# Retention, soft MoE and gated MLP on one core: the hand-over from the experts to the last product rewritten

## Chip, cores and metric

The kernel runs on one core of one Trainium2 chip. The metric is the device time of one execution in microseconds (us). Engines are named as in the profile: PE (matmuls) and PEld (its weight loads), DVE, ACT, POOL, and SP, whose queue issues most DMAs.

## The reference, cut to what matters

```python
attn = retention(q, k, v)                       # 4 x 8 heads x 768 tokens x 64
x = attn as 3072 tokens x 512
logits = x @ phi                                # 32 slots, 8 experts of 4 slots
d = softmax(logits over tokens); slot_input = d.T @ x
slot_out[e] = relu(slot_input[e] @ w1[e]) @ w2[e]
x = softmax(logits over slots) @ slot_out       # c @ slot_out
h = x @ w_in                                    # 512 -> 2048
out = (h * sigmoid(1.702 * h)) @ w_out          # 2048 -> 512
```

w_in and w_out are float64, and the kernel narrows them itself. The product x @ w_in is never formed through x: with G = slot_out @ w_in (32 x 2048), h is c @ G, so a block of h costs one matmul with the router's transposed weights c.

## The kernel before, in words

**Stages.** Attention runs first (to about 110 us of the span), then the experts in four pairs (`exp_w1` L484, `exp_t1` L498, `exp_w2` L507, `exp_t2` L523), then the last product, which fills the rest from about 159 us on.

**Experts.** `exp_w2(ep)` accumulates a pair's output in PSUM and copies it to `os` on ACT (L520). All pairs share one tile `eo` of two banks, pair `ep` taking bank `ep % 2` (L511). `exp_t2(ep)` turns `os` with 8 PE passes (`tq`) and lets DVE write the scaled result into `soT4`, which lies in tile A (L529). After pair 3, `make_gd(f)` (L536) can make 128 columns of G from `soT4` and `win`: 8 PE passes, an ACT copy (L541) and a DVE subtraction (L542) into `gst`.

**Narrowing.** A weight arrives as 64-bit words, and three DVE passes (`narrow`, L157: L160, L162, L164, called n1, n2, n3 below) make it float32. For a row block of w_out (`wout_ops`, L575), ACT then rounds a high part (L582) and POOL makes the low part (L585); later blocks are done in pairs by ACT and DVE. `wout_ops(0)` and `wout_ops(1)` are run by hand around the hand-over, `win_ops(0, 0, ...)` in two halves. Three buffers (`wq`, L86) hold raw weights, so a load on SP's queue waits until the pass n3 of an earlier raw tile is over.

**Router transposes.** `tr_cT(g)` (L422) turns the router weights of 512 tokens with four PE passes, and `copy_cT(g)` (L428) copies them into `cT` on ACT. Groups 0 to 2 are turned before the last product, groups 3 to 5 in its steps s = 7, 8 and 9 (L1143, L1144).

**Last product.** A unit u is a pair (b, f): a block b of 512 tokens and a row block f of w_out. `h_unit(u)` (L662) is one 128x512 matmul, then two ACT activations: `gh` (rounded, L674) and `gg` (L675). `lo_unit(u)` (L678) is the DVE subtraction `gl = gg - gh` (L680). `o_unit(u)` (L700) adds 12 matmuls of 512 columns into four accumulators: for each of four token tiles t, the terms (gh, w high), (gh, w low) and (gl, w high). Units 0 and 1 are block 0, 2 to 5 block 1, 6 to 9 block 2. Unit 0 runs term by term over the four tiles, all others tile by tile (L717, L724). The accumulators rotate over banks 0 to 4 (`acc_bank`), so the first unit of a block takes one free bank and three that the block before it must leave. `h_bank()` rotates over banks 5 to 7.

After a block's last unit, ACT copies the four accumulators into four buffers `sg` (L728, L732), and `store_sums()` (L690) has DVE subtract within two of them (L694) and sends all four to DRAM (L696). For block 0 these four DMAs are issued by ACT's own queue, in program order between its instructions. The next block's `sg` copies wait until the stores have landed.

**Order.** The order is written out by hand. Up to s = 4 it stands in L1085 to L1115. From s = 5 on, the loop at L1130 does `h_unit(s)`, a budget of weight preparation (`work`), `lo_unit(s)` and `o_unit(s - 2)`; at s = 5 `o_unit` is left out, as unit 3 is done already. `work(budget)` takes items off a queue, each with a cost written beside it, and carries an overdraft to the next call. Its items are, in order: the six narrowing passes of the third quarter of w_in (`b1`, L1042), w_out blocks 2 and 3 (`first_pair`, with two POOL passes at step 4), then the raw tiles wi1_0 and wi1_1 (three passes of 1024 columns each), and so on. At s = 5 block 0's sums are stored first thing (L1136).

**Idle passes.** `keep_warm(n)` (L480) issues n matmuls whose result nobody reads: 2, 1 and 2 of them (KW, L49) before `exp_t2(3)`, before `make_gd(0)` and before `h_unit(0)`.

Of the kernel before, what the change touches and what calls it, by code (L numbers as in the profile page):

```python
# [22 lines left out]
P = 128  # L23
# [22 lines left out]
I0 = 1  # L46
KTP = (0, 1, 2, 3, 8, 13, 16, 20)
PAD = 128
KW = (2, 1, 2)  # L49
BUD = 2.0  # L50
E0 = (1.2, 1.7, 1.7, 1.7, 2.2)
WL = (3, 2)
# [3 lines left out]
def retention_soft_moe_mlp(  # L56
# [418 lines left out]

    hT_t, H_p, O_p = {}, {}, {}

    kw = {}

    def keep_warm(n, cols=512):  # L480
        for _ in range(n):
            mm(kw["out"][:, 0:cols], lhsT=kw["in"][0], rhs=kw["in"][1][:, 0:cols], start=True, stop=True)

    def exp_w1(ep, k0=0, k1=KDM):  # L484
        if k0 == 0:
            H_p[ep] = ps.tile([P, 512], F32, tag=f"sc{ep % 2}", name=f"hp{ep}")
# [20 lines left out]
    def exp_w2(ep, k0=0, k1=4):  # L507
        if k0 == 0:
            if ep == 0:
                O_p["all"] = ps.tile([P, 2, 512], F32, tag="y", name="eo")  # L510
            O_p[ep] = O_p["all"][:, ep % 2]  # L511
        op, hT = O_p[ep], hT_t[ep]
        for kk in range(k0, k1):
            w = W["w2", ep, kk]
            for j in range(4):
                mm(op[32 * j:32 * j + 32, :], lhsT=hT[:, kk, 32 * j:32 * j + 32], rhs=w[:, j, :],  # L516
                   start=(kk == 0), stop=(kk == 3))
        if k1 == 4:
            os_ = xk.tile([P, 512], F32, tag="os", name=f"os{ep}", bufs=1)
            nc.scalar.copy(out=os_, in_=op)  # L520
            O_p[ep] = os_
# [53 lines left out]
    def wout_ops(f):  # L575
        r, c = f // 2, slice(f % 2 * DM, f % 2 * DM + DM)
        w = fr_tile(r)[:, c]
        h, l = w_t[r][:, 0, f % 2], w_t[r][:, 1, f % 2]
        n1, n2, n3 = narrow(w.bitcast(U32), raw_words(wo_t[r])[:, c])

        def hi():
            nc.scalar.copy(out=h, in_=w)  # L582

        def lo():
            nc.gpsimd.tensor_tensor(out=l, in0=w, in1=h.bitcast(F32), op=ALU.subtract)  # L585
            wh[f], wl[f] = h, l

        return [n1, n2, n3, hi, lo]
# [37 lines left out]
    def win_ops(j, z, k0=0, k1=KDM, f0=0, f1=256):  # L626
        raw = raw_t[j, z].bitcast(U32).rearrange("p k (f z) -> p k f z", z=2)
        if j not in win:
            win[j] = rw.tile([P, KDM, 512], F32, tag="win", name=f"win{j}", bufs=1)
        return narrow(win[j][:, k0:k1, 256 * z + f0:256 * z + f1].bitcast(U32), raw[:, k0:k1, f0:f1])  # L630
# [20 lines left out]
    def flat(i):  # L651
        return pb[:, i].rearrange("p z c -> p (z c)")
# [25 lines left out]
    def lo_unit(u):  # L678
        gg, gh, gl = g_hl[u]
        nc.vector.tensor_tensor(out=gl, in0=gg, in1=gh.bitcast(F32), op=ALU.subtract)  # L680
# [19 lines left out]
    def o_unit(u, t0=0, t1=4, terms=(0, 1, 2)):  # L700
        kind, (b, f) = seq[u]
        _, gh, gl = g_hl[u]
        whi, wlo = wh[f], wl[f]
        first = (b, f) in firsts
        last = kind == "p" and (b, f) in lasts
        final = u == NSEQ - 1
        ops = [(gh, whi), (gh, wlo), (gl, whi)]
        if first and 0 in terms:
            for t in range(t0, t1):
                acc[t] = acc_bank() if kind == "p" else flat(QBANK[t])  # L710

        def term(t, n):
            g, w = ops[n]
            mm(acc[t], lhsT=g[:, t * P:(t + 1) * P], rhs=w, start=first and n == 0,  # L714
               stop=n == 2 and (last or final or (u == NSEQ - 2 and t == 3)))

        if u == 0:  # L717
            for n in terms:
                for t in range(t0, t1):
                    term(t, n)  # L720
        if final:
            add_out(3, 0, 2, acc[3], store=False)
        for t in range(t0, t1 - 1 if final else t1):
            if u > 0:  # L724
                for n in terms:
                    term(t, n)
            if last:
                sg = fp.tile([P, DM], F32, tag="sg", name=f"sg{b}_{f}_{t}", bufs=4)  # L728
                if t % 2 and u == NP1 - 1:
                    nc.vector.tensor_copy(sg, acc[t])  # L730
                else:
                    nc.scalar.copy(out=sg, in_=acc[t])  # L732
                if u == NP1 - 1 and t in (1, 2):
                    s_load(0, t - 1)
                stores.append((scr[b][:, t], sg, t % 2 == 0, (b, f + 1) in seconds or b not in twice,
                               nc.sync if u == NP1 - 1 else nc.scalar if u == 1 else nc.gpsimd))
            if final:
                add_out(t, 0, 2, acc[t])
        if final:
            for n_, c in enumerate((slice(0, 256), slice(256, 512))):  # L740
                rest = flat(4 + n_)
                for n, (g, w) in enumerate(ops):
                    mm(rest[:, c], lhsT=g[:, 3 * P:4 * P], rhs=w[:, c], start=n == 0, stop=n == 2)
                add_out(3, n_, n_ + 1, rest)
# [71 lines left out]
    with tc.manual_schedule():  # L816
# [127 lines left out]
            WA[j] = wp.tile([P, 3, 2, 256], F32R, tag="w", name=f"wa{j}")  # L944
            WB[j] = wp.tile([P, 4, 2, 256], F32R, tag="w", name=f"wb{j}")
        load_wout(1)
        kw["in"] = cT[:, 0:128], cT
        nc.gpsimd.memset(selhl.bitcast(F32), 0.0)
        exp_t2(1)
        cp = [tr_cT(0, ps.tile([P, 4, P], F32R, tag="m", name="cp0", bufs=3))]  # L950
# [7 lines left out]
                    selhl[:, z, :, 64 * z + 32 * r:64 * z + 32 * r + 32], ident.rearrange("p (c s) -> p c s", c=4)  # L958
                )
        exp_w2(2)  # L960
        f0_ops = wout_ops(0)
        exp_w2(3, 0, 1)
        exp_t2(2)
        for fn in f0_ops:
            fn()
        exp_w2(3, 1, 4)
        cp = {g: tr_cT(g, ps.tile([P, 4, P], F32R, tag="m", name=f"cp{g}", bufs=3)) for g in (1, 2)}
        kw["out"] = ps.tile([P, 512], F32, tag="sc0", name="kw1")
        keep_warm(KW[0])
        exp_t2(3)  # L970
        for g in (1, 2):
            copy_cT(g, cp[g])
        w1_ops = win_ops(0, 0, f0=128)
        w1_ops[0]()
        w1_ops[1]()
        keep_warm(KW[1])
        make_gd(0, ps.tile([P, P], F32, tag="st", name="gd0"))
        w1_ops[2]()
        f1_ops = wout_ops(1)
        f1_ops[0]()  # L980
        f1_ops[1]()
        keep_warm(KW[2])
        xk_e.close()
        sm_e.close()
        ps_e.close()
# [53 lines left out]

            todo.append(make)  # L1040

        b1 = [x for p_ in zip(win_ops(0, 1, 0, 2), win_ops(0, 1, 2, 4)) for x in p_]  # L1042
        b1[-1] = used(b1[-1])
        todo.append(lambda: queue.extend(zip((0.4, 0.4, 0.7, 0.7, 0.7, 0.7), b1)))
        def first_pair():
# [36 lines left out]
                for fn in later.pop(x):  # L1082
                    fn()

        kw["out"] = flat(4)  # L1085
        h_unit(0)
        lo_unit(0)
        for fn in f1_ops[2:4]:
            fn()
        o_unit(0, terms=(0,))  # L1090
        make_gd(1, h_bank()[:, 0:P])
        f1_ops[4]()
        o_unit(0, terms=(1,))
        h_unit(1)
        work(E0[0])
        lo_unit(1)
        o_unit(0, terms=(2,))
        h_unit(2)
        work(E0[1])
# [30 lines left out]
        for s in range(5, NSEQ + 2):  # L1130
# [2 lines left out]
            u, nxt_ = s - 2, s + 1  # L1133
            if kind == "p":
                h_unit(s)
            if s == 5:  # L1136
                store_sums()
            if kind == "p":
                work(BUD - (0.8 if stores else 0))
                lo_unit(s)  # L1140
            store_sums()
            if kind == "p":
                if s in (7, 8, 9):  # L1143
                    copy_cT(s - 4, tr_cT(s - 4, h_bank().bitcast(F32R).rearrange("p (j t) -> p j t", j=4)))  # L1144
            if s == NP1 - 1:
                work(1000)
                for x in range(s, s + 9):
# [131 lines left out]
```

## Time and profile before

| | |
|---|---|
| median of 3 runs | 454.88 us (454.49 to 455.13) |
| profiled execution | 454.33 us |
| its span | 452.6 us (1.73 us lie around it) |
| busy: PE, DVE, ACT, POOL | 97%, 72%, 47%, 16% of the span |
| granted clock of TensorE | 1.00 (the full 2.4 GHz) |

The profile is of one execution. A row of the timeline gives the start in us from the span's beginning, the length, engine, source line, operation, out<-in, the shape and the count, and in brackets the idle time ahead of it with what ended that. Matmuls overlap, so the distance between starts is what one costs; a queue row (SPq, ACTq) is an issue of a DMA.

### The profile page before, as it was taken

What the parts mean: (1) busy time and instruction counts of PE and PEld (TensorE: products, weight loads), DVE (VectorE), ACT (ScalarE), POOL (GpSimd) and SP (SyncE); (2) the same over time, 40 slices, a digit from 0 to 9 for tenths busy, and PEclk for the clock granted to TensorE, in tenths of its full rate; (3) what the DMA queues carried; (4) which work ended last, traced back from release to release, by engine and by line L of the source; (5) the groups of instructions that cost most, each with busy time, mean ns of one, the idle gap of its engine ahead of it and who ended that gap; (6) DMA issues with size and microseconds to landing.
All of it is one profiled execution on the core that took longest, in us unless ns stands there. A gap on an engine that the chain in (4) does not pass through costs nothing.

```text
span 452.6 us, 10122 instructions
## 1 busy us (share of the span) xinstructions
PE 439.4 (97%) x4128; PEld 365.3 (81%) x4128; DVE 327.6 (72%) x624; ACT 214.2 (47%) x386; POOL 70.3 (16%) x81
## 2 busy tenths in 40 slices
PE   8999999999899989999999999999999999999996
PEld 5887877888333467788878878999999999999994
DVE  2455665765465488988778777798888999998835
ACT  2223233232121264673655657565666666665630
POOL 4344444443000112101130230000000000000000
PEclk9999999999999999999999999999999999999999
DMA  8999999999899657865576243503321333303102
GB/s 316 406 401 403 402 398 397 396 402 337 327 423 400 257 196 269 248 218 185 187 221 149 95 60 82 184 4 94 94 94 44 100 99 94 107 30 92 49 0 93
DMA packets 31630, 94.50 MB, mean 209 GB/s; under 512 B 3104, under 2 KB 10432, under 8 KB 28000
## 3 DMA queue, kind: packets, MB, share of 16 engines
q1 hardware_dynamic: 28176, 85.99, 51.6%
q0 software_dynamic: 2544, 6.46, 6.0%
q10 hardware_dynamic: 864, 1.41, 0.9%
q8 instruction: 32, 0.52, 0.5%
q14 instruction: 14, 0.11, 0.1%
HBM read 79.17 MB, written 14.68 MB: 207 GB/s over the span
## 4 chain that ended last, share of the span: by engine, by line
PE 87%; DMA 6%; DVE 5%; issue 1%; ACT 1%; DVEq 0%; ACTq 0%
PE pb L779 31%; PE pb L714 22%; DMA qt<-qt_dram 6%; PE sc L208 5%; PE y L257 4%; PE eo L516 3%; PE hp L491 3%; PE pb L753 3%; PE y L253 2%; PE pb L665 2%; PE xp L278 2%; PE st L265 1%; PE op L372 1%; PE wu L832 1%; PE kp L219 1%
## 5 line engine op out<-in xcount | busy, mean ns | idle before, releaser
L779 PE MATMUL pb<-wb,ghl 128*128 128x256 f32 x672 | 100.7, 283 | 0.0
L714 PE MATMUL pb<-wo_hl,gh 128*128 128x512 f32 x288 | 91.0, 398 | 0.7 <-ACT gh L674 0.7
L779 PEld LDWEIGHTS pb<-wb,ghl 128*128 128x128 f32 x672 | 89.5, 192 | 0.0
L779 PE MATMUL pb<-wa,ghl 128*128 128x256 f32 x504 | 78.9, 283 | 0.0
L779 PEld LDWEIGHTS pb<-wa,ghl 128*128 128x128 f32 x504 | 68.7, 192 | 0.0
L714 PEld LDWEIGHTS pb<-wo_hl,gh 128*128 128x128 f32 x288 | 53.5, 188 | 13.0 <-ACT gh L674 1.0
L768 DVE TENSOR_TENSOR ghl<-F,ghl 128x896 fp32r<-128x896 f32 x56 | 60.6, 1084 | 0.1
L756 ACT ACTIVATE F<-pb 128x512 f32<-128x512 f32 x56 | 33.5, 598 | 52.2 <-PE pb L753 52.2
L714 PE MATMUL pb<-wo_hl,gl 128*128 128x512 f32 x144 | 56.6, 397 | 1.2 <-DVE gl L680 1.2
L764 ACT CAST ghl<-F 128x896 fp32r<-128x896 f32 x56 | 52.3, 934 | 1.4 <-DVE F L760 1.4
L212 DVE TENSOR_TENSOR pt<-sc,ca_t 128x512 f32<-128x512 f32 x44 | 28.3, 686 | 19.2 <-PE sc L208 19.2
L680 DVE TENSOR_TENSOR gl<-gg,gh 128x512 fp32r<-128x512 f32 x36 | 24.8, 688 | 16.3 <-ACT gg L675 16.2
L674 ACT ACTIVATE gh<-pb 128x512 fp32r<-128x512 f32 x36 | 21.7, 603 | 29.6 <-PE pb L665 27.6
L714 PEld LDWEIGHTS pb<-wo_hl,gl 128*128 128x128 f32 x144 | 27.2, 189 | 8.6 <-DVE gl L680 2.1
L758 DVE TENSOR_TENSOR F<-F 128x256 f32<-128x256 f32 x56 | 23.6, 422 | 14.0 <-ACT F L756 13.8
L234 POOL TENSOR_TENSOR tb<-ca_t 128x512 f32<-128x512 f32 x19 | 19.9, 1048 | 42.8 <-DVE xT L269 42.8
L208 PEld LDWEIGHTS sc<-qt,ktv 64*128 64x128 f32 x320 | 19.8, 187 | 7.8 <-issue 4.5
L267 ACT COPY s_sb<-st 128x256 f32<-128x256 f32 x20 | 7.5, 372 | 38.5 <-PE st L265 38.5
L208 PE MATMUL sc<-qt,ktv 64*128 64x128 f32 x320 | 23.7, 284 | 1.3 <-DMA qt<-qt_dram 1.1
L257 PE MATMUL y<-pt,vt 128*64 128x128 f32 x352 | 24.1, 279 | 0.0
L226 POOL TENSOR_TENSOR vt<-ktv,ca_t 128x512 f32<-128x512 f32 x20 | 20.9, 1042 | 12.2 <-PE xp L278 6.5
L753 PE MATMUL pb<-cT,gst 128*128 128x256 f32 x112 | 22.6, 284 | 0.0
(188 smaller groups left out, 653.2 us busy)
## 6 DMA issues: line engine op xcount, KB each, us to landing
w<-w_dram SPq DMA_DIRECT2D x36, 512.0 KB, 7.4
w<-w_dram SPq DMA_DIRECT2D x14, 1024.0 KB, 8.3
ktv<-ktv_dram SPq DMA_DIRECT2D x20, 512.0 KB, 8.3
wi<-w_in_dram SPq DMA_DIRECT2D x7, 1024.0 KB, 5.0
wo<-w_out_dram SPq DMA_DIRECT2D x7, 1024.0 KB, 4.9
scr<-sg POOLq DMA_DIRECT2D x24, 256.0 KB, 3.5
pr<-scr SPq DMA_DIRECT2D x12, 512.0 KB, 5.0
qt<-qt_dram SPq DMA_DIRECT2D x21, 256.0 KB, 6.4
```

Of the source, the lines that this page charges most:

```text
L208: mm(sc[hh][:, a, :], lhsT=kT[hh * D:(hh + 1) * D, a, :], rhs=q_[hh * D:(hh + 1) * D, a, :], start=True, stop=True)
L212: nc.vector.tensor_tensor(out=pt[hh], in0=sc[hh], in1=mask[:, None, :].to_broadcast([P, NP, P]), op=ALU.mult)
L257: mm(out_(a, hh ^ (a & 1)), lhsT=vt[:, 2 * a + (hh ^ (a & 1)), :], rhs=pt[hh ^ (a & 1)][:, a, :], start=(c == 0 and a < 2), stop=True, ski ...
L674: nc.scalar.activation(out=gh, in_=hp, func=AF.Gelu_apprx_sigmoid)
L680: nc.vector.tensor_tensor(out=gl, in0=gg, in1=gh.bitcast(F32), op=ALU.subtract)
L714: mm(acc[t], lhsT=g[:, t * P:(t + 1) * P], rhs=w, start=first and n == 0, stop=n == 2 and (last or final or (u == NSEQ - 2 and t == 3)))
L753: mm(hp[:, 256 * z:256 * z + 256], lhsT=gst[:, (f + z) * P:(f + z + 1) * P], rhs=cT[:, 256 * blocks[e]:256 * blocks[e] + 256], start=z == ...
L756: nc.scalar.activation(out=F[:, 0:4].rearrange("p q t -> p (q t)"), in_=hp, func=AF.Gelu_apprx_sigmoid)
L758: tt(out=F[:, 4:6], in0=F[:, 0, None].to_broadcast([P, 2, P]), in1=F[:, 1:3], op=ALU.subtract)
L764: nc.scalar.copy(out=GHL[k][:, 0], in_=F_[k][:, 1:8])
L768: nc.vector.tensor_tensor(out=GHL[k][:, 1], in0=F_[k][:, 1:8], in1=GHL[k][:, 0].bitcast(F32), op=ALU.subtract)
L779: mm(pv[:, p], lhsT=ghl[:, n // 2, g], rhs=wf[:, n % 2], start=j == j0[e] and n == 0 and i in (4, 0), stop=j == NSP - 1 and n == 2, skip_g ...
```

## The change

Six things change.

- `keep_warm`, KW and the five idle passes are gone.
- Pair 3 of the experts gets a PSUM bank of its own for its output.
- The narrowing of w_out block 0 is moved ahead of `exp_t2(2)`; the second half of `win_ops(0, 0)` comes ahead of the rest of pair 3; the first two passes of `wout_ops(1)` come before `make_gd(0)`'s subtraction, the third after it.
- `tr_cT(3)` goes behind `exp_t2(3)`, `make_gd(1)` and `tr_cT(4)` go right behind `h_unit(0)`, `h_unit(1)` between the first two terms of unit 0, `tr_cT(5)` ahead of its third term; steps 7 to 9 lose their transposes.
- Unit 1 runs term by term, as unit 0 did; its four `sg` copies follow when the loop over terms is over.
- Block 0's sums are stored at s = 6 behind `lo_unit(6)`, not at s = 5 ahead of the work, and the budget at s = 6 is 0.8 smaller.

```diff
-KW = (2, 1, 2)
...
-            O_p[ep] = O_p["all"][:, ep % 2]
+            O_p[ep] = O_p["all"][:, ep % 2] if ep < 3 else ps.tile([P, 512], F32, tag="sc0", name="eo3")
...
-        if u == 0:
+        if u < 2:
             for n in terms:
                 for t in range(t0, t1):
                     term(t, n)
         if final:
             add_out(3, 0, 2, acc[3], store=False)
         for t in range(t0, t1 - 1 if final else t1):
-            if u > 0:
+            if u > 1:
                 for n in terms:
                     term(t, n)
...
         exp_w2(2)
-        f0_ops = wout_ops(0)
+        f0_ops, f1_ops = wout_ops(0), wout_ops(1)
+        for fn in f0_ops[0:3]:
+            fn()
         exp_w2(3, 0, 1)
         exp_t2(2)
-        for fn in f0_ops:
+        for fn in f0_ops[3:5] + win_ops(0, 0, f0=128):
             fn()
         exp_w2(3, 1, 4)
         cp = {g: tr_cT(g, ps.tile([P, 4, P], F32R, tag="m", name=f"cp{g}", bufs=3)) for g in (1, 2)}
-        kw["out"] = ps.tile([P, 512], F32, tag="sc0", name="kw1")
-        keep_warm(KW[0])
         exp_t2(3)
-        for g in (1, 2):
+        cp[3] = tr_cT(3, ps.tile([P, 4, P], F32R, tag="sc1", name="cp3"))
+        for g in (1, 2, 3):
             copy_cT(g, cp[g])
-        w1_ops = win_ops(0, 0, f0=128)
-        w1_ops[0]()
-        w1_ops[1]()
-        keep_warm(KW[1])
+        b1 = [x for p_ in zip(win_ops(0, 1, 0, 2), win_ops(0, 1, 2, 4)) for x in p_]
+        for fn in f1_ops[0:2]:
+            fn()
         make_gd(0, ps.tile([P, P], F32, tag="st", name="gd0"))
-        w1_ops[2]()
-        f1_ops = wout_ops(1)
-        f1_ops[0]()
-        f1_ops[1]()
-        keep_warm(KW[2])
+        f1_ops[2]()
...
         h_unit(0)
+        make_gd(1, h_bank()[:, 0:P])
+        cp4 = tr_cT(4, cp_bank())
         lo_unit(0)
-        for fn in f1_ops[2:4]:
-            fn()
+        f1_ops[3]()
         o_unit(0, terms=(0,))
-        make_gd(1, h_bank()[:, 0:P])
         f1_ops[4]()
+        h_unit(1)
+        copy_cT(4, cp4)
         o_unit(0, terms=(1,))
-        h_unit(1)
         work(E0[0])
         lo_unit(1)
+        copy_cT(5, tr_cT(5, cp_bank()))
         o_unit(0, terms=(2,))
...
             if kind == "p":
                 h_unit(s)
-            if s == 5:
+            if kind == "p":
+                work(BUD - (0.8 if stores and s > 5 else 0))
+                lo_unit(s)
+            if s > 5:
                 store_sums()
-            if kind == "p":
-                work(BUD - (0.8 if stores else 0))
-                lo_unit(s)
-            store_sums()
-            if kind == "p":
-                if s in (7, 8, 9):
-                    copy_cT(s - 4, tr_cT(s - 4, h_bank().bitcast(F32R).rearrange("p (j t) -> p j t", j=4)))
```

## Rows read from the trace of the kernel before

**Rows 1.** Chain of work that ended last, 200 to 212 us: start, us, what

```profile
204.96 0.23 PE pb L665
205.19 2.81 PE pb L714 x12
```

**Rows 2.** Timeline of PE, 149 to 160 us

```profile
149.58 1.06 PE L516 MATMUL eo<-w,hT 128*32 128x512 f32 x8 [0.76 <-ACT os L520]
...
155.00 0.69 PE L482 MATMUL kw<-cT 128*128 128x512 f32 x2
155.53 0.95 PE L527 MATMUL tq<-selo,os 128*128 128x8 f32 x8
...
156.87 1.16 PE L538 MATMUL gd<-win,A 128*128 128x128 f32 x8
...
158.80 0.47 PE L665 MATMUL pb<-cT,gst 128*128 128x512 f32 x1 [0.31 <-DVE gst L542]
```

**Rows 3.** Timeline of ACT: copy of pair 3, sg copies of units 1 and 5

```profile
154.47 0.59 ACT L520 COPY os<-eo 128x512 f32<-128x512 f32 x1
...
166.16 2.69 ACT L732 COPY sg<-pb 128x512 f32<-128x512 f32 x4 [0.45 <-PE pb L714]
...
182.26 0.60 ACT L732 COPY sg<-pb 128x512 f32<-128x512 f32 x1
...
182.73 0.62 ACT L732 COPY sg<-pb 128x512 f32<-128x512 f32 x1
```

**Rows 4.** Timeline of DVE, 151 to 189 us

```profile
151.67 0.29 DVE L529 TENSOR_TENSOR A<-tq,zr 128x128 f32<-128x128 f32 x1 [3.36 <-PE tq L527]
...
170.59 0.23 DVE L553 TENSOR_TENSOR Gl<-pb,Gh 128x64 fp32r<-128x64 f32 x1
...
174.70 0.69 DVE L680 TENSOR_TENSOR gl<-gg,gh 128x512 fp32r<-128x512 f32 x1 [1.48 <-ACT gg L675]
175.31 2.96 DVE L694 TENSOR_TENSOR sg<-sg 128x256 f32<-128x256 f32 x2
178.19 1.21 DVE L162 SCALAR_TENSOR_TENSOR win<-wi,win 128x1024 uint32<-128x1024 uint32 x1
...
180.58 0.68 DVE L680 TENSOR_TENSOR gl<-gg,gh 128x512 fp32r<-128x512 f32 x1
...
183.04 0.69 DVE L680 TENSOR_TENSOR gl<-gg,gh 128x512 fp32r<-128x512 f32 x1
...
187.72 0.76 DVE L694 TENSOR_TENSOR sg<-sg 128x256 f32<-128x256 f32 x2
```

**Rows 5.** Busy us by stretch: PE, PEld, DVE, ACT, POOL, clock, DMA share, GB/s

```profile
150.00:154.00 4.00, 4.00 (x40) 1.65 (x32) 2.01 (x4) 0.21 (x1) 0.00 (x0) 1.00 1.05 416
154.00:158.00 4.00, 3.95 (x32) 3.28 (x29) 1.32 (x3) 1.97 (x4) 1.29 (x1) 1.00 0.06 23
```

**Rows 6.** Timeline of PE, 164 to 174 us

```profile
164.19 0.39 PE L665 MATMUL pb<-cT,gst 128*128 128x512 f32 x1
...
170.87 0.30 PE L561 MATMUL pb<-Gl,selhl 128*128 128x64 f32 x1 [0.20 <-DVE Gl L553]
...
173.16 0.39 PE L665 MATMUL pb<-cT,gst 128*128 128x512 f32 x1
```

**Rows 7.** Timeline of POOL, 175 us: low parts of w_out blocks 2 and 3

```profile
175.25 2.73 POOL L585 TENSOR_TENSOR wo_hl<-fr,wo_hl 128x512 fp32r<-128x512 f32 x2 [11.51 <-ACT wo_hl L582]
```

**Rows 8.** Block 0's stores: first issue; landing of all on scr; ACT's four

```profile
176.86 0.34 ACTq L696 DMA_DIRECT2D scr<-sg  x1
...
DMA to landing us min/median/max: 2.4/3.6/8.2
...
scr<-sg ACTq DMA_DIRECT2D x4, 256.0 KB, 2.8
```

**Rows 9.** Timeline of PE, 179 to 186 us: a transpose, unit 6's second tile

```profile
179.68 0.45 PE L425 MATMUL pb<-csb 128*128 128x128 f32 x4
179.97 0.70 PE L714 MATMUL pb<-wo_hl,gh 128*128 128x512 f32 x2
...
185.03 0.63 PE L714 MATMUL pb<-wo_hl,gh 128*128 128x512 f32 x2
```

More of the change, by code (lines that the diff above doesn't have):

```diff
@@ L476, in retention_soft_moe_mlp @@
     hT_t, H_p, O_p = {}, {}, {}
[L478 to L482, printed above, removed]
     def exp_w1(ep, k0=0, k1=KDM):
@@ L946, in retention_soft_moe_mlp @@
         load_wout(1)
-        kw["in"] = cT[:, 0:128], cT
         nc.gpsimd.memset(selhl.bitcast(F32), 0.0)
@@ L1040, in add_g @@
             todo.append(make)
-        b1 = [x for p_ in zip(win_ops(0, 1, 0, 2), win_ops(0, 1, 2, 4)) for x in p_]
         b1[-1] = used(b1[-1])
@@ L1083, in due, with cp_bank @@
                     fn()
-        kw["out"] = flat(4)
+        def cp_bank():
+            return h_bank().bitcast(F32R).rearrange("p (j t) -> p j t", j=4)
         h_unit(0)
+        make_gd(1, h_bank()[:, 0:P])
+        cp4 = tr_cT(4, cp_bank())
         lo_unit(0)
-        for fn in f1_ops[2:4]:
-            fn()
+        f1_ops[3]()
         o_unit(0, terms=(0,))
-        make_gd(1, h_bank()[:, 0:P])
         f1_ops[4]()
+        h_unit(1)
+        copy_cT(4, cp4)
         o_unit(0, terms=(1,))
-        h_unit(1)
         work(E0[0])
         lo_unit(1)
+        copy_cT(5, tr_cT(5, cp_bank()))
         o_unit(0, terms=(2,))
```

## Prediction

> **What bounds the kernel.** I read the page's busy shares and slices first: PE is busy for 97% of the span. Then the chain of work that ended last, which shows what a step costs: from about 182 us on it is PE alone, one unit being an `h` matmul and twelve more, 0.23 + 2.81 = 3.04 us, so 0.234 us each with nothing between [rows 1]. Time saved or lost on PE ahead of that stretch therefore moves the end one for one. Third, the timelines of each engine between 148 and 186 us, where PE still waits: for a copy of the experts' output [rows 2], for the chain behind `tq` and G, for `gl`. The change acts only there, so I lay its work out again with the durations of the rows and read off how much earlier, or later, the packed stretch begins. I count against the profiled execution: 454.33 us, of which 452.6 are span and 1.73 lie around it. The median of the runs is 0.55 above it.
>
> **Own bank, and `tq` of pair 3.** Pair 3's first eight passes started at 149.58, 0.76 late, when the copy of pair 2's output was over, because the tile is shared [rows 2]. With its own bank they start at 148.8; `tq` of pair 2 still needs that copy, and starts at 149.6 instead of 149.58 + 1.0 = 150.6. All behind it moves by 1.0: the copy of pair 3 from 154.47 to 153.5, over at 154.1 [rows 3]. `tq` of pair 3 follows it directly. Before, it started at 155.53, because two idle passes from 155.00 on stood ahead of it [rows 2]: now 154.15, a gain of 1.4. The other three idle passes lie inside the waits from `tq` to G and from G to `h_unit(0)`, so they free nothing: those distances stay 156.87 - 155.53 = 1.34 and 158.80 - 156.87 = 1.93 [rows 2]. `h_unit(0)` comes at 157.4. `tr_cT(3)`, 179.97 - 179.68 = 0.29 us [rows 9], fits into the first wait.
>
> **Narrowing moved up.** DVE has 3.36 us idle ahead of 151.67 [rows 4], which covers the three passes for w_out block 0. The second w_in product needs raw data that arrives late: data flows at 416 GB/s until about 154 and hardly at all after that, and behind this half another 0.5 and 1 MB stand in the queue, 3.6 us at that rate [rows 5]. So its data is in near 151 to 152.5; three passes of at most 0.7 end by 154.6, before `tq` needs DVE at 155.1. If that cover were gone, the scaling of `soT4`, and G, would wait by as much. SP, queued behind the third pass with the next raw loads, goes earlier by some 5 us; nobody waits for those.
>
> **Units 0 and 1.** Between `h_unit(0)` and `h_unit(2)` PE now has two `h` (0.47), G's second part (at most 1.16 [rows 2]; 0.8 if its passes keep their distance), two transposes (0.58) and twelve matmuls (2.81): 4.7 to 5.0, and it no longer waits for `gh` or G. ACT and DVE work beside it, at 0.6 to 0.7 for 512 columns [rows 3, 4] and some 0.3 for G's 128: `gh` is there at 158.5, G's part at 159.5, `gl` at 160.2, each before PE asks. `h_unit(2)` starts at 162.2, before 164.19 [rows 6]: 2.0 gained with two transposes more inside. Unit 1 term by term no longer waits for `gl`, and PE is through at 165.2. But its first accumulator is complete only after nine of the twelve matmuls, at 164.8, and the four `sg` copies on ACT follow each other at 182.73 - 182.26 = 0.47 [rows 3], where before they came at PE's pace during the unit, the last over at 166.16 + 2.69 = 168.85 [rows 3]. Now the last is over at 164.8 + 3 x 0.47 + 0.6 = 166.8. Queued behind it on ACT are `gh`, `gg` and the round part of G for unit 3, and DVE's low part `Gl`, for which PE waits. That took 170.59 + 0.23 - 168.85 = 1.97 [rows 3, 4]; `Gl` is ready at 168.8, PE goes on at 168.85 instead of 170.87 [rows 6], and `h_unit(4)` is at 171.15, not 173.16. So of the lead of 2.9 that unit 1 had, 2.0 remains.
>
> **Block 0 stored later: the term that decides.** With that, DVE's `gl` of unit 4 starts at 172.7 (before: 174.70 [rows 4]). Two low parts on POOL follow 0.55 later, 2.73 us long [rows 7]. Before, DVE's subtractions for the stores stood there and took 2.96 us for the two [rows 4], as long as POOL was busy; undisturbed two take 0.76 [rows 4]. So POOL's passes cost DVE 2.2 us. Now the second and third narrowing passes of wi1_0 stand there. No row shows such a pass beside POOL. The least that it can lose is nothing, the most 2.2, as the subtractions did; they are the nearest row (also two inputs in SBUF), and I take 2.2. The Trainium skill, SBUF — State Buffer, section "SBUF: two separate sides", says that a VectorE operation with two SBUF inputs and a GpSimd operation lock each other out for a whole instruction; by that rule it is the same 2.2, and no gain from moving the subtractions.
>
> DVE's way from `gl` of unit 4 to `gl` of unit 6 was 183.04 - 174.70 = 8.34 [rows 4], with the subtractions. Without their own 0.76 it is 7.6: `gl` of unit 6 starts at 180.3, the first subtraction ends at 180.3 + 0.6 + 0.4 = 181.3 (the smaller budget at s = 6 still lets the same two passes through before it, as both have a positive rest). ACT's queue waits for it from 177 on with `gh` of unit 7 behind it. The first store is issued at 181.35 and lands 2.4 us later (176.86 shows such an issue; 2.4 is the least of all on that tile, 2.8 the median of ACT's four [rows 8]): 183.75. Only then can ACT copy unit 5's first accumulator, in 0.6, because the four `sg` buffers hold block 0 until their stores land. Unit 6's second tile needs that accumulator's bank: 184.45.
>
> PE would be there at 171.15 + 44 matmuls x 0.234 = 181.45, or 181.9 with a wait of 0.45 for `gl` of unit 5. It stands for 2.5 us, about the whole gain. Before, the same matmul started at 185.03 [rows 9]: 0.6 gained there. The other tiles follow at PE's pace: a tile is 3 x 0.234 = 0.7, and the stores are issued closer than that (0.34 each [rows 8]). The transposes of the last two groups cost nothing more later: one was ahead of 185.03, the other gives 0.3 [rows 9]. Work is late by 0.8 of budget for the rest, which is covered by DVE's idle time; if that were gone, the start of the last stage would slip. **Sum: 0.6 + 0.3 = 0.9.** 454.33 - 0.9 is 453.4 as a profiled run, 454.0 as a median. A landing of 2.8 gives 0.5, so this case is 453.8 to 454.7.
>
> **Rivals.**
> - *The passes of wi1_0 lose little beside POOL.* Then stores start up to 2.2 earlier, the wait shrinks to PE's own 181.45 or to 0.8, and the gain is 2.0 (half of the loss) to 3.0: 451.9 to 452.9. For it: no row shows these passes blocked. Against it: both subtractions were.
> - *The stores land late: a wait in place of the one removed, and slower.* They share the DMA engines with a raw load of 1 MB, issued near 178 when wi1_0 is narrowed. At the median of all stores, 3.6 [rows 8], the gain is 0.9 - 1.2 = -0.3: 455.2, still no change that shows. From a landing of 4.2 on it is slower by over 0.9; at 5.0 the result is 456.6. For it: the longest took 8.2 [rows 8]. Against it: ACT's four had a median of 2.8, with another raw load ending beside them.
> - *The clock falls.* With the idle passes gone and PE standing for 2.5 us, matmuls after it could run at 1.2 GHz, 0.47 each, one unit costing 3.04 more: 457. Against it: the granted clock is 1.00 in every stretch, with waits of up to 0.76; but none is as long as 2.5. The Trainium skill, TensorE: Matmul & The Clock Gate, section "What's actually happening", says that an idle engine falls to the lower level; by that rule 457, if the wait is long enough.
>
> **Chances.** The sum 0.47: its 0.9 is just what a measurement here can tell from no change (0.2%, 0.9 us), so I split it, 0.28 faster and 0.19 the same. DVE unhindered 0.21, faster. Stores at about 3.6, 0.19, the same. Stores at over 4.2, 0.09, and the clock, 0.04, slower. Faster 0.49, same 0.38, slower 0.13. The range from 452.3 to 455.3 leaves out the slower cases and the best third of the unhindered one; the likeliest case alone has 453.8 to 454.7.
>
> **What would show it.** Right: no wait of pair 3's passes for a copy; `h_unit(0)` 1.4, `h_unit(4)` 2.0 earlier; narrowing passes of 1024 columns beside POOL at over 2 us instead of 1.2; ACT idle for over 4 us until DVE's L694; then one PE wait of about 2.5 us in unit 6's second tile, ended by an `sg` copy; no other new wait; the packed stretch ahead by under 1 us. Wrong: no PE wait there (then about 3 us are gained), one of over 3.4 us (slower), or a granted clock under 1.00.

## The result, and the profile after: slower by 0.7%

The changed kernel takes 457.26 us (median of 5 runs, 456.86 to 459.53), beside 454.49 us (5 runs) for the kernel before: ratio 1.0073, 95% interval 1.0044 to 1.0102. Forecast were 454.0 us and a range of 452.3 to 455.3: outside the range, with the other sign.

| | before | after |
|---|---|---|
| median | 454.49 us | 457.26 us |
| profiled execution, its span | 454.33, 452.6 us | 459.53, 457.7 us |
| busy: PE, DVE, ACT, POOL | 97%, 72%, 47%, 16% | 96%, 72%, 47%, 15% |
| mean granted clock | 1.00 | 0.994 |

The profiled execution is the slowest of the five. 0.8 us of it arise ahead of everything that the change touches: pair 3's first eight passes stand at about 149.6 (32 of 40 passes after 145.99, below), where 148.8 was forecast with no wait. I take these 0.8 off where a position is compared with the forecast.

PE's timeline of the changed kernel (start us, length, and in brackets the idle time before with what ended it):

```profile
145.99 4.50 PE L509 MATMUL eo<-w,hT 128*32 128x512 f32 x40
...
158.24 0.50 PE L658 MATMUL pb<-cT,gst 128*128 128x512 f32 x1 [0.68 <-DVE gst L535]
...
169.84 0.30 PE L554 MATMUL pb<-Gl,selhl 128*128 128x64 f32 x1 [0.58 <-DVE Gl L546]
...
172.12 0.39 PE L658 MATMUL pb<-cT,gst 128*128 128x512 f32 x1
...
179.49 0.50 PE L707 MATMUL pb<-wo_hl,gl 128*128 128x512 f32 x1 [0.21 <-DVE gl L673]
...
186.28 1.14 PE L707 MATMUL pb<-wo_hl,gh 128*128 128x512 f32 x2 [3.26 <-ACT sg L725]
...
191.38 0.73 PE L707 MATMUL pb<-wo_hl,gh 128*128 128x512 f32 x2 [2.09 <-ACT sg L725]
```

Up to 180 us the timeline is the forecast one. The 40 passes of pairs 2 and 3 have no gap (before: 0.76 [rows 2]); `h_unit(0)` at 158.24 is 157.4 + 0.8; `h_unit(4)` at 172.12 is 171.3 + 0.8 (forecast 171.15). Then there are two waits for `sg` copies where one of 2.5 was forecast: 3.26 at unit 6's second tile, 2.09 at its fourth. What ACT does there:

```profile
177.03 0.62 ACT L668 ACTIVATE gg<-pb 128x512 f32<-128x512 f32 x1
182.27 2.35 ACTq L689 DMA_DIRECT2D scr<-sg  x4
184.66 0.60 ACT L667 ACTIVATE gh<-pb 128x512 fp32r<-128x512 f32 x1 [7.01 <-DVE win L163]
185.16 0.59 ACT L668 ACTIVATE gg<-pb 128x512 f32<-128x512 f32 x1
185.63 0.59 ACT L725 COPY sg<-pb 128x512 f32<-128x512 f32 x1
187.00 0.59 ACT L725 COPY sg<-pb 128x512 f32<-128x512 f32 x1 [0.78 <-DMA scr<-sg]
190.74 1.07 ACT L725 COPY sg<-pb 128x512 f32<-128x512 f32 x2 [3.15 <-DMA scr<-sg]
```

Before, the four `sg` copies followed each other from 182.26 on, the first two 0.47 us apart [rows 3]. Now ACT does nothing for 7 us: its queue stands at the first store, issues all four (2.35 us), and only then `gh` and `gg` of unit 7 run and the first copy. By then the first store has landed, so that copy (185.63) waits for nothing; the releaser that the row of `gh` names, a DVE pass that nothing here reads, is only what ended nearby. Copies two and three wait for landings, the third for 3.15 us. The chain of work that ended last goes through that landing:

```profile
183.72 6.94 DMA scr<-sg
...
190.74 0.59 ACT sg L725
```

The DMA view of 172 to 192 us (KB each, median us from issue to landing) shows what else was under way: ACT's four stores, whose median was 2.8 before [rows 8], and a raw load of 1 MB, which SP issues at 183.73 when the third narrowing pass of wi1_1 frees its buffer.

```profile
scr<-sg ACTq DMA_DIRECT2D x4, 256.0 KB, 5.6
wi<-w_in_dram SPq DMA_DIRECT2D x1, 1024.0 KB, 6.7
```

The stores land 2.52, 4.29, 6.94 and 6.96 us after their issue. DVE and POOL did what the sum said:

```profile
174.28 2.31 DVE L161 SCALAR_TENSOR_TENSOR win<-wi,win 128x1024 uint32<-128x1024 uint32 x1
176.63 2.20 DVE L163 SCALAR_TENSOR_TENSOR win<-wi,win 128x1024 uint32<-128x1024 uint32 x1
...
181.81 0.75 DVE L687 TENSOR_TENSOR sg<-sg 128x256 f32<-128x256 f32 x2
```

The two narrowing passes beside POOL's low parts take 2.31 and 2.20 instead of 1.21 [rows 4], 2.1 lost for 2.2 forecast, and the subtractions take 0.75 for both. The granted clock, by stretch (the columns of [rows 5]):

```profile
186.00:190.00 4.00, 3.01 (x6) 1.58 (x6) 2.30 (x3) 0.81 (x2) 0.00 (x0) 0.57 0.96 335
190.00:194.00 4.00, 2.62 (x11) 2.17 (x12) 1.16 (x3) 3.05 (x6) 0.00 (x0) 1.00 0.06 22
```

After the first wait PE runs at 1.2 GHz for most of a stretch (0.57), 0.43 us a matmul instead of 0.23. Here this costs nothing: tile four starts when the store has landed, and a faster PE would only have waited longer.

### The profile page after: what moved, and what is told of

Its sections match the earlier page's. It is cut to its first block, busy times and chain, and to the rows that moved or that the text cites. A ratio compares the mean times of both kernels' runs of the same rounds, so it can differ in the third digit from the quotient of the medians.

```text
span 457.7 us, 10112 instructions
## 1 busy us (share of the span) xinstructions
PE 440.1 (96%) x4123; PEld 365.4 (80%) x4123; DVE 328.6 (72%) x624; ACT 213.9 (47%) x386; POOL 70.6 (15%) x81
## 4 chain that ended last, share of the span: by engine, by line
PE 84%; DMA 9%; DVE 3%; issue 2%; ACT 1%; DVEq 0%; ACTq 0%
PE pb L772 31%; PE pb L707 21%; DMA qt<-qt_dram 8%; PE sc L207 4%; PE hp L484 3%; PE y L256 3%; PE eo L509 3%; PE pb L746 3%; PE y L252 2%; PE pb L658 2%; DMA scr<-sg 2%; PE xp L277 2%; PE st L264 1%; PE wu L825 1%; PE op L371 1%
```

## The experiments

Each kernel was timed against the kernel before on its own chip, so ratios are compared.

| kernel | median us (runs) | ratio, 95% interval |
|---|---|---|
| the change | 457.26 (5) | 1.0073 (1.0044 to 1.0102) |
| early_store | 452.63 (11) | 0.9963 (0.9950 to 0.9975) |
| late_only | 461.50 (6) | 1.0164 (1.0137 to 1.0191) |
| own_buffers | 456.18 (12) | 1.0033 (1.0014 to 1.0053) |
| own_buffers_pool | 453.44 (6) | 0.9972 (0.9960 to 0.9983) |
| pool_queue | 461.08 (4) | 1.0148 (1.0122 to 1.0174) |
| late_load | 457.11 (9) | 1.0062 (1.0038 to 1.0086) |
| late_pass | 456.38 (6) | 1.0039 (1.0023 to 1.0054) |
| no_idle | 454.89 (12) | 1.0013 (0.9994 to 1.0032) |
| idle_back | 452.77 (6) | 0.9966 (0.9955 to 0.9978) |
| store_s4 | 452.43 (7) | 0.9965 (0.9952 to 0.9977) |
| unit1_tiles | 451.92 (6) | 0.9939 (0.9925 to 0.9953) |
| s4_tiles | 452.23 (5) | 0.9954 (0.9941 to 0.9968) |
| tiles_bank | 451.15 (6) | 0.9926 (0.9912 to 0.9940) |

### Which part costs: early_store and late_only

early_store is the change without the late store:

```diff
             if kind == "p":
                 h_unit(s)
+            if s == 5:
+                store_sums()
             if kind == "p":
-                work(BUD - (0.8 if stores and s > 5 else 0))
+                work(BUD - (0.8 if stores else 0))
                 lo_unit(s)
-            if s > 5:
-                store_sums()
+            store_sums()
```

> The changed kernel with one part undone: block 0's sums are stored at s = 5 ahead of the work again, with the old budgets. Theory A (the four sg buffers are held until late stores land): the two PE waits for sg copies at unit 6 (3.26 and 2.09 us) are gone, the granted clock is 1.00 to the end, PE waits about 1 us for gl of unit 5 instead, and the time is 451.6 to 452.8 us. Theory B (the loss comes from the missing idle passes: PE cools at the hand-over): the clock still falls and the time stays at 456 or more.

late_only is the kernel before with the late store alone (the same lines the other way round):

> The kernel before with only the late store of block 0. Theory A: laid out from the rows of before, gl of unit 6 is at 182.3, the first store is issued near 183.4 and lands near 185.9, the third is issued beside the load of wi2_0 and takes about 7; unit 6's second tile starts 1.5 us late and its fourth 3 to 5.5 us late: 457.5 to 460 us. Theory B: the idle passes are kept, so 454 to 455, with the clock at 1.00.

Measured: 0.9963 and 1.0164. The late store is the whole loss: on top of the other parts it costs 457.26 - 452.63 = 4.6 us (on two chips, where the kernel before took 454.49 and 454.36), by itself 461.50 - 454.36 (the kernel before on that chip) = 7.1. The other parts gain 1.7. In early_store no wait for an `sg` copy is left; the stores land in 2.6 to 3.2 us, and the largest wait in this part is for the `gl` of unit 5, behind the subtractions beside POOL. DVE's timeline of early_store has the subtractions:

```profile
173.68 2.95 DVE L687 TENSOR_TENSOR sg<-sg 128x256 f32<-128x256 f32 x2
```

PE's timeline has the wait:

```profile
179.69 0.50 PE L707 MATMUL pb<-wo_hl,gl 128*128 128x512 f32 x1 [1.00 <-DVE gl L673]
```

and its DMA view, 172 to 192 us, the stores:

```profile
scr<-sg ACTq DMA_DIRECT2D x4, 256.0 KB, 3.0
```

late_only came out above what was expected. Its PE timeline says why:

```profile
186.81 0.53 PE L425 MATMUL pb<-csb 128*128 128x128 f32 x4 [3.33 <-ACT gg L675]
...
193.63 0.54 PE L425 MATMUL pb<-csb 128*128 128x128 f32 x4 [2.57 <-ACT gg L675]
```

The router transposes still stand in steps 7 to 9. Each takes a bank that ACT must have read, and ACT stands at the stores, then at their landings. PE waits here 3.33 + 0.34 + 2.57 us, with none of the lead that the other parts give. So moving the transposes out of these steps saved the change from worse.

### ACT's queue or the buffers: own_buffers, own_buffers_pool, pool_queue

Two things hold the first `sg` copy: ACT's queue, with four issues, `gh` and `gg` ahead of it, and the four buffers, full until block 0's stores land. own_buffers gives block 0's sums four other buffers (a weight buffer that is free then; its type makes the copy round these sums):

```diff
...
-                sg = fp.tile([P, DM], F32, tag="sg", name=f"sg{b}_{f}_{t}", bufs=4)
+                if u == 1:
+                    sg = WB[4][:, t].rearrange("p a d -> p (a d)")
+                else:
+                    sg = fp.tile([P, DM], F32, tag="sg", name=f"sg{b}_{f}_{t}", bufs=4)
```

> The changed kernel, stores as late as there, but block 0's four sums go into a tile that is idle until much later (its type rounds block 0's two partial sums on the copy), so unit 5's sg copies find free buffers. Theory A: no PE wait for an sg copy, clock 1.00, 452.0 to 453.6 us, with up to 1 us of PE wait for gl of unit 7, as ACT's queue still stands until the stores are issued. Theory C (it is ACT's queue, blocked by the four issues, and not the buffers): PE still waits over 2 us around units 6 and 7 and the time stays over 455.5.

own_buffers_pool also issues these four stores from POOL's queue:

```diff
-                               nc.sync if u == NP1 - 1 else nc.scalar if u == 1 else nc.gpsimd))
+                               nc.sync if u == NP1 - 1 else nc.gpsimd))
```

> As the run with own buffers (block 0's two partial sums rounded on the copy), but the four late stores are issued by POOL's queue instead of ACT's. Theory C2 (the first wait of 3.1 to 3.3 us is ACT's queue: four issues, then gh and gg of unit 7, then the first sg copy): the wait is gone, ACT runs gh of unit 7 near 179, and the time is 451.3 to 452.4 us. Rival (the sg copies are late for another reason, the accumulators or DVE's order): a PE wait of over 2 us stays at unit 6 and the time over 454.5.

pool_queue has this second edit alone, with the four buffers:

> The changed kernel with its four buffers and its late stores, but the four stores are issued from GpSimd's queue and not from ScalarE's. It separates the two causes of the first wait. Theory Q+B (ScalarE's queue and the four buffers each hold PE up on their own): ScalarE no longer stands for 7 us with gh of unit 7 behind the issues, but the first sg copy of block 1 still has to wait until the first store has landed, near 182.2 + 3 = 185.2, and the later ones for landings of up to 8 us; PE waits about 2.5 us at unit 6's second tile and again at a later one, 456.0 to 458.5. Theory Q alone (only the queue costs): no sg wait, as with both removed, 453.4 (452.8 to 454.2).

In own_buffers (ratio 1.0033), PE's timeline keeps the first wait:

```profile
185.44 0.72 PE L707 MATMUL pb<-wo_hl,gh 128*128 128x512 f32 x2 [3.13 <-ACT sg L728]
```

and ACT's shows what is ahead of the copies:

```profile
181.56 2.22 ACTq L689 DMA_DIRECT2D scr<-wb  x4
183.83 0.60 ACT L667 ACTIVATE gh<-pb 128x512 fp32r<-128x512 f32 x1 [6.88 <-DVE win L163]
...
184.80 2.06 ACT L728 COPY sg<-pb 128x512 f32<-128x512 f32 x4
```

No copy depends on a landing any more, all four run in a row, and the second wait is gone. The first is still 3.13: it is ACT's queue. With POOL's queue as well (0.9972) it goes too, although these stores take 3.0 to 8.3 us to land: nobody waits for them. The time, 453.44, is above the 451.3 to 452.4 expected. Its profile loses time far ahead of the change: PE's wait for a load ends at 18.02 after 1.84 us, the granted clock of the next four us is 0.57, and `h_unit(0)` comes 2.0 later than in own_buffers. Of the kernel's six executions five have a mean clock of 0.995 or 0.996; the one at 1.00 took 452.00. The copies in ACT's timeline of own_buffers_pool, at PE's pace:

```profile
181.33 2.70 ACT L728 COPY sg<-pb 128x512 f32<-128x512 f32 x4
```

In pool_queue, where ACT's queue is free and the buffers are not, PE's timeline has

```profile
185.25 1.22 PE L707 MATMUL pb<-wo_hl,gh 128*128 128x512 f32 x2 [3.31 <-ACT sg L725]
...
187.95 1.22 PE L707 MATMUL pb<-wo_hl,gh 128*128 128x512 f32 x2 [1.05 <-ACT sg L725]
...
190.69 1.22 PE L707 MATMUL pb<-wo_hl,gh 128*128 128x512 f32 x2 [1.10 <-ACT sg L725]
```

and ACT's says what for:

```profile
184.61 0.59 ACT L725 COPY sg<-pb 128x512 f32<-128x512 f32 x1 [5.63 <-DMA scr<-sg]
187.31 0.59 ACT L725 COPY sg<-pb 128x512 f32<-128x512 f32 x1 [2.11 <-DMA scr<-sg]
190.06 1.07 ACT L725 COPY sg<-pb 128x512 f32<-128x512 f32 x2 [2.16 <-DMA scr<-sg]
```

So each cause is enough for a first wait of over 3 us, and removing one alone brings little or, with landings of 3.1, 5.2, 7.4 and 7.3 us from POOL's queue, makes it worse. It came out at 461.08, above the 456.0 to 458.5 that were expected, as the clock also stayed low. Its stretches:

```profile
186.00:190.00 4.00, 2.54 (x6) 1.01 (x4) 0.00 (x0) 0.59 (x1) 0.00 (x0) 0.50 0.82 304
190.00:194.00 4.00, 3.31 (x8) 2.64 (x9) 1.84 (x4) 3.15 (x6) 0.28 (x1) 0.50 0.01 2
```

### Why the stores land late: late_load and late_pass

late_load puts off the request for the next load, the 1 MB of wi2_0, by two units in program order:

```diff
+                if (j, z) == (1, 1):
+                    third = n[2]
+                    n[2] = lambda: (third(), at(now[0] + 2, lambda: loads.pop()()))
...
```

> The changed kernel with the raw load of wi2_0 put off by about two units, so that block 0's stores have the DMA engines to themselves. Theory D (the stores land late because that load of 1 MB runs beside them): the third and fourth store land within 3.5 us instead of 7, the second PE wait (2.09 us) is gone, the first one stays at 2.5 to 3.3, and the time is 454.8 to 455.9 us. Theory E (stores from ACT's queue are slow by themselves when four are in flight): landing stays at 5 to 7 us and the time at 456.8 or more.

It tells nothing on its question: SP's queue holds nothing else, so the load was issued at 184.64 all the same, as soon as its buffer was free, and the stores landed in 2.4, 3.8, 4.7 and 6.5 us, the last again late (the wait ahead of the fourth tile was 0.41 in this profile). late_pass puts off the pass that frees the buffer:

```diff
+                if (j, z) == (1, 1):
+                    third = n[2]
+                    n[2] = lambda: at(now[0] + 1, third)
```

> The changed kernel, but the third narrowing pass of wi1_1, which frees the buffer for the 1 MB load wi2_0, comes on VectorE behind the low part of unit 7 and no longer ahead of it. That low part waits for what stands behind the four stores in ScalarE's queue, so this time the load really is issued later: near 187 us in place of 183.73, when stores that land alone would be in. Theory L (the load beside the stores makes the last three land late): all four land in 2.4 to 3.2 us, the wait of 2.09 us ahead of unit 6's fourth tile goes or is under 0.5, the wait of about 3.3 us ahead of its second tile stays; 455.0 to 455.8. Rival (stores of a tile in this form and place land late whatever runs beside them): landings of 4 to 7 us again, both waits as they were; 457.0 to 457.6. If the time doesn't go down although the landings are short, the second wait belongs to ScalarE's order and not to the buffers.

Now the load is issued at 186.71, behind the stores, and these land in 2.41, 2.94, 2.96 and 3.06 us. The DMA view of late_pass, 176 to 190 us:

```profile
scr<-sg ACTq DMA_DIRECT2D x4, 256.0 KB, 2.9
```

Its ACT timeline, where the copies no longer wait:

```profile
184.71 2.23 ACT L725 COPY sg<-pb 128x512 f32<-128x512 f32 x4
```

The second wait is gone, as expected of the load; the first stays. The load beside the stores is what made the last two take 7 us in the change. The Trainium skill, DMA: Bandwidth & Descriptors, section "Issuing engines are not separate DMA queues", says that DMAs from all issuing engines run on the same 16 DMA engines and interleave. The trace agrees: ACT's last two stores took 6.94 and 6.96 us beside SP's load, 2.96 and 3.06 ahead of it. It also says that issuing from more engines saves only sequencer time, usually small beside the transfer. In this kernel it is that time which holds the first tile up: 2.35 us of issues in front of ACT's work.

The time fell only to 1.0039, not to the 455.0 to 455.8 expected, since the clock takes part back. Its stretches:

```profile
186.00:190.00 4.00, 4.00 (x11) 3.14 (x10) 3.96 (x7) 1.93 (x4) 0.00 (x0) 0.50 0.58 168
190.00:194.00 4.00, 4.00 (x36) 3.04 (x39) 1.65 (x2) 1.09 (x2) 2.18 (x4) 0.84 0.87 235
```

From unit 6's second tile to the `h` of unit 9 it takes 189.36 - 185.35 = 4.01 us, in own_buffers, at full clock, 187.65 - 185.44 = 2.21; to the next `h` it is 5.03 for 4.13: together 2.7 us lost. It was the slowest of its six runs (457.65; the others 456.26 to 456.75).

### Idle passes: no_idle, idle_back

no_idle is the kernel before with `KW = (0, 0, 0)`; idle_back is early_store with two idle passes between `make_gd(0)` and `h_unit(0)`.

> The kernel before without its five idle passes, nothing else changed. By the layout only the two ahead of the last expert product free time: 0.4 us, 453.9 to 454.2 against 454.36, clock 1.00. Theory F (clock falls at the hand-over in some executions): the median is 454.3 or more, the spread wider than before's, with some executions at 455.5 or more.

> The kernel with the early store, and two idle passes put back into the wait between G's first part and unit 0 (0.68 us of PE idle). Theory F (without idle passes the clock falls at the hand-over in some executions, which costs over 1 us there): the slower executions of the early-store kernel (3 of 11 above 453.0) become rarer, the fastest stay at 452.2 to 452.4, median 452.2 to 452.6. Rival G (the idle passes do nothing for the clock): the same spread and median as the early-store kernel; if the passes push unit 0 back, 0.1 to 0.3 slower.

By the median neither can be told from its base: 1.0013 (0.9994 to 1.0032) beside 1, and 0.9966 beside 0.9963. In idle_back the two passes only fill the wait ahead of `h_unit(0)`, 0.31 instead of 0.68.

But no_idle did what theory F said of it: median 454.89, spread from 453.82 to 457.30. Four of its five executions at a mean granted clock of 0.999 took 453.82 to 454.06, about the 0.4 less that the layout gives, the fifth 454.66; its seven at 0.990 to 0.996 took 454.82 to 457.30, five of them over 456. The kernel before has 1 of 20 executions at 0.996 or less on the same chip, 2 of 76 beside all the experiments. So in that kernel the passes help to keep the clock up, which by the median pays for their 0.4 us. Where it falls without them is not shown, as the one profiled execution of no_idle is at 0.999. Two profiles of other kernels without the passes, store_s4 and late_load, have a stretch of 1.2 GHz right at the hand-over. unit1_tiles, s4_tiles and tiles_bank, also without them, have none of 17 executions below 0.997. In the change the removal is not the loss, as early_store lacks the passes too.

### Earlier still, and unit 1 tile by tile: store_s4, unit1_tiles, s4_tiles

store_s4 calls `store_sums()` ahead of `work(E0[4])` and issues from POOL's queue:

> The changed kernel with block 0's sums stored ahead of the work of s = 4, where DVE idles 1.5 us before gl of unit 4, and issued by POOL's queue, idle until its low parts near 174. Theory H (in the early-store kernel the subtractions stand beside POOL's low parts, 2.95 us instead of 0.76, and delay gl of unit 5 by 1.0 us on PE): two subtractions take 0.76, the wait for gl of unit 5 shrinks to under 0.3, and the time is 451.3 to 452.0 us. Rival I (the passes of wi1_0 stand there then and lose the same 2 us, and POOL's issues push its low parts back): the wait stays at 0.5 to 1.0 and the time at 452.2 to 453.

0.9965, as early_store. The subtractions come ahead of POOL's low parts, but a narrowing pass meets those instead and takes 3.95 us; the wait for `gl` is 0.65, not 1.00. The stores take 7.2 to 7.4 us, beside a load, and harm nobody.

unit1_tiles is early_store with unit 1 tile by tile again:

```diff
-        if u < 2:
+        if u == 0:
...
-            if u > 1:
+            if u > 0:
```

> The kernel with the early stores (all of the change but the late store), and unit 1 goes tile by tile as before the change, not term by term. The prediction said that term by term gives PE a lead of 2.9 us of which 0.9 is lost again, since the four sg copies then stand behind unit 1 and hold up Gl. Theory U (term by term is worth little): unit 1 waits at most 0.5 for gl, the 0.58 us wait for Gl goes, and what is gained or lost ahead is taken up by the wait of 1.00 us for gl of unit 5: 452.2 to 453.0, the same as 452.6. Rival (PE needs gl of unit 1 over 1.5 us before it is there): a new wait of 1.5 to 2.5 us in unit 1, of which 1.0 is taken up later: 453.2 to 454.2.

0.9939, better than early_store and below the range that I gave. PE's timeline of unit1_tiles:

```profile
168.46 0.30 PE L554 MATMUL pb<-Gl,selhl 128*128 128x64 f32 x1 [0.20 <-DVE Gl L546]
...
178.90 0.51 PE L707 MATMUL pb<-wo_hl,gl 128*128 128x512 f32 x1 [1.01 <-DVE gl L673]
```

The wait for `Gl` is 0.20 instead of 0.58, since the copies run during the unit, and the wait for `gl` of unit 5 does not grow: ACT and DVE come earlier too. So term by term is worse here than tile by tile: from `h_unit(0)` to `h_unit(4)` it is 13.87 us in early_store and 13.39 in unit1_tiles, 0.48 of the 0.7 between their medians. s4_tiles joins both edits:

> The two versions that beat both kernels, put together: block 0 stored ahead of the budgeted work of unit 4, from GpSimd's queue, and unit 1 tile by tile. If the 0.7 us of the second adds to the first, whose wait for gl of unit 5 was 0.65 and not 1.00: 451.4 (451.0 to 451.8). Rival: unit 1 tile by tile ends later on PE, but its first tile complete earlier; the wait for gl of unit 5 hangs on the two low parts on GpSimd, which stand in either order of the stores, and takes up what else is gained: 451.8 to 452.4, the same as unit 1 tile by tile alone.

0.9954: they don't add. store_s4's order is no better on top of it.

### What was left over: tiles_bank

Between 255 and 292 us of the kernel before, at the last part of G, every kernel above but no_idle falls back by 0.44 to 0.67 us against it. early_store has there, in PE's timeline, a wait that the kernel before hasn't:

```profile
271.24 0.51 PE L746 MATMUL pb<-cT,gst 128*128 128x256 f32 x2 [0.39 <-ACT gst L555]
```

tiles_bank is unit1_tiles with one empty request for a bank:

```diff
+            if s == 10:
+                h_bank()
             if kind == "p":
                 h_unit(s)
```

> The kernel with the early stores and unit 1 tile by tile, and the rotation over banks 5 to 7 is moved on by one at step 10. The change asks for one bank of this rotation less than the kernel before (three transposes in steps 7 to 9 are gone, two others and G's part come earlier, one uses another bank), so that from there on each later user stands in another bank. Theory R: the last part of G now lies in the bank that the first matmul of the split stage uses, which therefore waits for ACT's copy of it, 0.39 us at 270.5 where the kernel before had no wait; with the rotation as before that wait goes, the distance to the kernel before stays the same across that place and about 0.6 us comes back: 451.3 (450.9 to 451.6). Rival (the wait is due to ACT or to a weight that comes late, whichever bank is used): the wait stays or another takes its place, 451.9.

0.9926: the wait goes, and the lead over the kernel before stays at 3.26 us through that place, where unit1_tiles falls from 3.16 to 2.50. PE's timeline of tiles_bank:

```profile
269.80 0.40 PE L746 MATMUL pb<-cT,gst 128*128 128x256 f32 x2
```

That holds for the kernels with the early store. In the changed kernel the same 0.55 has another look: the smaller budget at s = 6 has moved G's work, and its second part comes right behind its first and one `h`, with no unit between, so PE waits in small steps for ACT's and DVE's copies. PE's timeline of the changed kernel:

```profile
276.48 0.51 PE L658 MATMUL pb<-cT,gst 128*128 128x512 f32 x1
276.93 0.33 PE L553 MATMUL pb<-Gh,selhl 128*128 128x128 f32 x1
277.26 0.33 PE L554 MATMUL pb<-Gl,selhl 128*128 128x128 f32 x1
```

late_only, with the old rotation and the smaller budget, has the same order and loses 0.44. So in the changed kernel most of the 0.55 goes with the budget; no run set that back there alone.

At 451.15 us (451.08 to 451.69) this is the best version, below both kernels: all of the change but the late store and unit 1 term by term, with the rotation set right.

## Why the prediction was wrong

**Own bank, `tq`, narrowing moved up: right.** `h_unit(0)` came 1.36 earlier (the 0.8 taken off), for 1.4 in the sum; the wait ahead of it is 0.68. None of the moved passes is waited for.

**Units 0 and 1: right in size for the change, not seen as improvable.** `h_unit(4)` came 1.84 earlier (forecast 2.0), and PE's wait is for `Gl` behind the `sg` copies, as said. unit1_tiles shows that the old order of unit 1 kept more: its `h_unit(4)` is at 170.74 and early_store's at 171.53, with `h_unit(0)` at 157.35 and 157.66: 0.48 better.

**POOL beside the narrowing passes: right** (2.1 lost for 2.2), so the rival "the passes of wi1_0 lose little beside POOL" falls. The rule of SBUF — State Buffer, section "SBUF: two separate sides", in the Trainium skill holds here: 2.31 and 2.20 us for passes of 1.2.

**Block 0 stored later: the step that failed.** The prediction put it so: "The first store is issued at 181.35 and lands 2.4 us later [...] Only then can ACT copy unit 5's first accumulator", and "The other tiles follow at PE's pace". Both halves fail.
- The first copy waits longer for ACT's queue than for the landing: four issues (2.35 us), `gh` and `gg` stand between the first issue at 182.27 and the copy at 185.63, 3.36 us, while the first store landed after 2.52, near the forecast 2.4. Unit 6's second tile came at 186.28 for 184.45 + 0.8: 1.0 late. The sentence before it in the prediction had `gh` of unit 7 queued behind the store, and then priced neither it nor the other three issues. own_buffers shows this half alone. The landing would have held the copy too (pool_queue, 3.31), but here only to 184.79. The trace of before had a price for the four issues: 2.28 us from the first at 176.86 [rows 8] to the end of the other three, in part a wait for the second subtraction, which ends at 178.27. ACT's timeline of before:

```profile
177.24 1.90 ACTq L696 DMA_DIRECT2D scr<-sg  x3
```

- The other tiles do not follow at PE's pace. The third store is issued when the 1 MB load is, and took 6.94 us; tile four came at 191.38 for a forecast 186.65 (with the 0.8): 4.7 late, of which 3.7 are this landing's. late_pass shows this half alone. The rival "the stores land late" had a load of 1 MB beside the stores, but the wrong load and the wrong store. Its load, issued near 178, is at 178.86 in the trace and lands 4.91 later, ahead of the first store's landing; the one that counts is the next, which the third pass of wi1_1 releases at 183.73. And it priced one landing for the first tile, 2.4 to 5.0, where that of the third counts.

**What was costed at nothing: wrong by 0.5.** The prediction held that the transposes "cost nothing more later" and that the 0.8 of budget "is covered by DVE's idle time". In the early-store kernels the first costs 0.66, through the bank rotation (tiles_bank); in the changed kernel the second moves G's work to a place without cover, and 0.55 are lost there.

The sum against the profiled execution then closes: 453.4 forecast + 0.8 ahead of the change + 1.0 + 3.7 + 0.5 = 459.4, measured 459.53. The median is 2.3 below that execution; only one of the five runs has a profile, so how the others divide is not shown.

**The clock** fell, which had been given 457 and a chance of 0.04. The Trainium skill, TensorE: Matmul & The Clock Gate, section "What's actually happening", says that an idle engine falls to the lower level. Of six profiled executions with a wait of over 3 us, four show 1.2 GHz soon behind it or already in it (the change, late_load, late_pass, pool_queue), two don't (own_buffers 3.13, late_only 3.33). In the change it hid under the second wait, in late_pass it cost 2.7. All five executions of the change have a mean of 0.993 to 0.995, so the clock fell in each; only one shows where.

**What stays open.** own_buffers spreads from 454.42 to 458.67, and the spread goes with the clock: its five executions at a mean of 1.00 took 454.42 to 455.05, its seven at 0.990 to 0.996 took 456.10 to 458.67. Where the clock fell in these is not shown, as the one profiled is at 1.00. Nor is it shown why a wait of over 3 us lowers the clock in one execution and not in the next.

## What to carry to other kernels

A store is priced by the whole queue that issues it: all its issues and everything in program order behind them on that engine, and then, where its buffer is used again, by the landing of the last store that the next user needs, with the loads that are released meanwhile beside it. Where two causes are each enough for one wait, removing either alone brings little; test them together and apart. When executions of one kernel fall into groups, sort them by their granted clock before taking two medians for the same. A change that asks a rotating buffer for one place less shifts every later user; look at where each lands.

## What the runs showed of the hardware that was not expected

- Block 0's stores of 256 KB landed in 2.4 to 3.2 us where no load of 1 MB was issued until the last of them was nearly in (before, early_store, late_pass), and the last of the four in 6.5 to 7.0 (ACT's queue) or 7.3 to 8.3 us (POOL's) beside such a load. Not explained: in the profile of no_idle they took 4.2 to 4.8 us, though the load before them landed at 177.0 and the next was issued at 180.24.
- The four issues in ACT's queue took 2.2 to 2.35 us, not four times the 0.34 of the first [rows 8], and in that time ACT did nothing else.
- The granted clock also fell to half with no long wait ahead: in the profiled executions of store_s4 and late_load at about 157.5 us, at the hand-over, where no wait is over 0.7 us.
